# Dense keys and values, and a batch's attention in four groups of 64x64 products

## Chip, cores, metric

One core of a Trainium2 chip runs the whole kernel. The metric is the device time of one execution in microseconds (us), taken over several runs; lower is better.

## What is computed

Eight batches of attention with eight heads each (576 positions, head size 64), then a gated feed-forward block on the 4608 rows of 512 that the heads make together. Heads 0 to 3 see a plain window of the last 32 positions, heads 4 to 7 a window of 128 of which only every fourth position counts.

```python
scores = scale * np.matmul(q, k.transpose(0, 1, 3, 2))
mask_plain = (rel >= 0) & (rel < 32)
mask_dil = (rel >= 0) & (rel < 32 * 4) & (rel % 4 == 0)
attn = softmax(where(mask, scores, -1e9))
x = matmul(attn, v)                       # 4608 x 512 after the heads are put side by side
out = (gelu(x @ w_gate) * (x @ w_val)) @ w_out    # inner width 1536
```

## The kernel before

**Chunks.** The feed-forward block works on nine chunks of 512 rows. Each has a gate stage of 96 matmuls of 512 columns (`ffn1_part`, L636: 12 blocks of the inner width, gate and value, four contraction pieces `kc`) and an output stage of 48 (`ffn2`, L643: four row blocks `tb` of 12). ScalarE (ACT) makes gelu, `g` (L805); VectorE (DVE) multiplies it with the value product, `u` (L810). Results leave through `store` (L651), by ACT (`e`) or DVE (`w`), and a DMA on the SP queue.

**Attention** is done for pairs of heads, called units: unit n belongs to batch n // 4, and each batch has two plain and two dilated units (`pair`, L357: batches 2 and 3 have the dilated ones first). A unit passes these steps, each a letter in the program strings:
- S, scores (L459, L473): 9 blocks of 64 keys by up to 96 queries, for both heads.
- P, the exponential on ACT (L508); M, the mask on DVE (L513).
- D, denominators (L566): a product with ones. N, numerators (L570): a product with the values.
- A, the reciprocal by ln and exp on ACT (L606, L608), or T and B, by transposes on DVE (L594, L611).
- X, the product of numerator and reciprocal into `xT` (L627), one 128-row piece for each unit of a batch: piece `pair(n)` is what the gate matmuls of contraction piece kc read.

**Storage.** For batches 1 to 7, keys and values of the two heads of a unit stand as 128x128 blocks with the heads on the diagonal (or, for odd units, off it: `odd`, L268) and zeros elsewhere. A full 128x128 product then gives both heads. GpSimd (POOL) makes them: `zero` (L199), the spreads (L278 to L289) and the casts of the values (L262), from dense loads. When two units are emitted together (`emit_tiles`, L448), the kernel leaves the zeros out: each product is cut to two 64x64 products, and the even unit uses the diagonal quarters of TensorE, the odd one the other two. Batch 0 has dense keys and uses 64x64 products with a bias for its mask.

**Order.** Nothing is scheduled by a compiler: each engine runs its instructions in the order in which the program gives them. For every chunk c, `gates[c]` and `outs[c]` are strings that `run_program` (L786) walks: a number issues so many matmuls of the chunk's list, `S8@0+S9@6` emits the scores of two units together with their PSUM banks, `e1@2` evicts row block 1 of chunk 2, G and E load ACT's table for gelu or for exp and ln, V, F, H, R start loads. Batch c+1 is computed mostly in the output stage of chunk c; its last numerators, and for batches 6 and 7 more, lie in the gate stages. `firsts` orders the first 16 gate matmuls, so that pieces of `xT` that come late are read late.

**Loads.** Weights come by DMAs on POOL's queue (`load_w`, `load_wo`), with the queries and keys of batches 0 and 1. Values of batch 1 come by SP's queue into `stage` (`load_v`, L245 plain, L250 and L254 dilated); the first of them is held until the second piece of the output weights has landed (`gated`, L163). Later batches: F loads and casts q and k (L291), H transposes them by DMA (L273) and fetches the values (`load_rest`, L317).

**PSUM** has eight banks of 512 columns; gate stages use two pairs of banks in turn, the output stage two, and attention the rest (`win`, `base_of`).

Of the kernel before, what the change touches and what calls it, by code (L numbers as in the profile page):

```python
# [21 lines left out]
def kernel(  # L22
# [29 lines left out]
    NB2 = S // BK  # L52
    BIG = 60000.0
# [19 lines left out]
    ones_two = const.tile([P, P], F16, tag="ones_two")  # L73
# [8 lines left out]

    vraw = [const.tile([P, 4 * NB2 * P], F16, tag=f"v{i}", name=f"v{i}") for i in range(3)]
    qraw = [const.tile([P, 2 * 640 + 8 * NCL + 4 * NB2 * P], F16, tag=f"q{i}", name=f"q{i}") for i in range(2)]
    stage = const.tile([P, 3840], F32, tag="stage")
    s16 = const.tile([P, 4608], F16, tag="s16")
    dense = const.tile([P, 1280 + 8 * NCL], F16, tag="dense")
# [90 lines left out]
    def blocks(t, plain):  # L178

        return t[:, (1 - plain) * 2 * NB2 * P : (2 - plain) * 2 * NB2 * P].rearrange("p (e c) -> p e c", c=P)  # L180

    def views(b):

        raw = qraw[b % 2]
        kt = raw[:, 1280 + 8 * NCL :]
        return (
            raw[:, 0:1280].rearrange("p (g c) -> p g c", g=2),
            raw[:, 1280 : 1280 + 8 * NCL].rearrange("p (g r i) -> p g r i", g=2, r=4),
            blocks(kt, 1),
            blocks(kt, 0),  # L190
            blocks(vraw[b % 3], 1),
            blocks(vraw[b % 3], 0),
        )
# [5 lines left out]
    def zero(t, eng=nc.gpsimd, gs=(0, 1), swap=1):  # L199

        for x in range(2):
            g = gs[0]
            part = t[64 * x : 64 * x + 64].bitcast(F32)
            first = 32 - 32 * (x ^ (g * swap))
            step = NB2 * 64 + swap * (32 if x else -32) * (1 - 2 * g)
            eng.memset(at2(part[:, NB2 * g], first, [[step, len(gs)], [64, NB2], [1, 32]]), 0.0)  # L206
# [49 lines left out]
    def cast_v(dst, i, gs=(0, 1), swap=1):  # L256

        st = st_of(i)[:, 0:1152].rearrange("p (e d) -> p e d", d=D)
        for g in gs:
            for x in range(2):  # L260
                at = slice(NB2 * g, NB2 * g + NB2)
                nc.gpsimd.tensor_copy(dst[half_of(x), at, half_of(x, g * swap)], st[half_of(x), at])  # L262
# [12 lines left out]
    kdp = dense[:, 0:1280].rearrange("p (g c) -> p g c", g=2)  # L275
    kdd = dense[:, 1280 : 1280 + 8 * NCL].rearrange("p (g r i) -> p g r i", g=2, r=4)

    def spread(eng, dst, src, x, g):  # L278

        half = half_of(x)  # L280
        eng.tensor_copy(dst[half, :, :, half_of(x, g)], src[half])  # L281

    def spread_two(dst, src, x):

        half, step = half_of(x), NB2 * P + (-64 if x else 64)
        n = src.shape[2] // 64
        base = dst[half, 0, 64 * x : 64 * x + 1]
        out_ = bass.AP(tensor=base.tensor, offset=base.offset, ap=[base.ap[0], [step, 2], [P, n], [1, 64]])
        nc.gpsimd.tensor_copy(out_, src[half].rearrange("p g (j c) -> p g j c", c=64))  # L289

# [10 lines left out]
    def spread_plain(kp):  # L301
        for x in range(2):
            spread_two(kp, kdp[:, :, 0:S], x)

    def spread_dil(kd, rest):
        for x in range(2):
            for g in range(2):
                spread(
                    nc.gpsimd,
                    kd[:, NB2 * g : NB2 * g + 8].rearrange("p (r i) c -> p r i c", r=4),  # L310
                    kdd[:, g, :, 0:P].rearrange("p r (i c) -> p r i c", c=64),
                    x,
                    g,
                )
            spread_two(kd[:, 8:], rest, x)

    def load_rest(b):  # L317
        qp, qd, kp, kd, vp, vd = tiles["two", b] = views(b)
        turn(qp.rearrange("p g (k c) -> p (g k) c", c=P), s16[:, 0:1280])
        turn(kdp.rearrange("p g (k c) -> p (g k) c", c=P), s16[:, 1280:2560])  # L320
        turn(qd.rearrange("p g r i -> p (g r) i")[:, :, 0:P], s16[:, 2560:3584])
        turn(kdd.rearrange("p g r i -> p (g r) i")[:, :, 0:P], s16[:, 3584:4608])
        for plain in (0, 1):
            load_v(b, 2 - plain, plain)
        spread_plain(kp)
        spread_dil(kd, kdp[:, :, S:640])
        nc.gpsimd.tensor_copy(qd[:, :, :, P:NCL], qp[:, :, S:640].rearrange("p g (i r) -> p g r i", r=4))
        cast_v(vd, 2)
        cast_v(vp, 1)

    def v_first(g):

        dst = vraw[0][:, 2304:3456].rearrange("p (e d) -> p e d", d=D)
        for x in range(2):
            half = slice(64 * x, 64 * x + 64)
            nc.gpsimd.dma_start(
                out=dst[half, 8 * g : 8 * g + 8].rearrange("p (i r) d -> p i (r d)", r=4),
                in_=v[0, HK + 2 * g + x, 0 : 4 * P].rearrange("(i p r) d -> p i (r d)", i=2, r=4),
            )
            if g == 0:  # L340
                nc.gpsimd.dma_start(out=dst[half, 16:18], in_=v[0, HK + x : H : 2, S - 64 : S].rearrange("g p d -> p g d"))
# [35 lines left out]
    def turn_first(n, bank, eng):  # L377
# [11 lines left out]
        if kind:  # L389
            dst = (kdd if t else views(b)[1])[:, hp].rearrange("p r (i e) -> p r i e", e=2)  # L390
            src = col.rearrange("p (e r i) -> p r i e", e=2, r=4)
        else:
            dst = (kdp if t else views(b)[0])[:, hp, 0:S].rearrange("p (i r) -> p i r", r=6)
            src = col.rearrange("p (r i) -> p i r", r=6)
        copy(("dve", "act")[eng], dst, src)
        if kind and t:
            rest = kdp[:, hp, S:640].rearrange("p (i r) -> p i r", r=8)
            copy(("dve", "act")[eng], rest, col.rearrange("p (r i) -> p i r", r=8)[:, 64:R8, :])
        if b and n % 4 == 3:
            if kind:  # L400
                spread_dil(views(b)[3], kdp[:, :, S:640])
            else:
                spread_plain(views(b)[2])
# [4 lines left out]
    def win(n, i):  # L408
        return (2048 + 1024 * i) % 4096 + (0 if is_plain(n) else 80)
# [38 lines left out]
    def emit_tiles(*lists):  # L448

        queues, at = [list(mms) for mms, _ in lists], [0.0] * len(lists)  # L450
        while any(queues):
# [3 lines left out]
            for x in range(2):  # L455
                rows, cols = half_of(x), half_of(x, lists[i][1])
                nc.tensor.matmul(o[cols], lhs[rows, cols], rhs[rows], start=st, stop=end, skip_group_check=True)  # L457

    def two_s_mms(n, bank):  # L459

        b, hp = n // NHP, n % 2
        qp, qd, kp, kd, _, _ = tiles["two", b]
# [3 lines left out]
        for e, c0, t0, w in two_blocks(n):  # L466
            rhs = qp[:, hp, t0 : t0 + w] if is_plain(n) else qd[:, hp, e // 2, t0 - NCL * (e // 2) : t0 - NCL * (e // 2) + w]
            mms.append((psf[:, base + c0 : base + c0 + w], (kp if is_plain(n) else kd)[:, NB2 * hp + e, :], rhs, True, True))
        if not is_plain(n):
            mms.append((psf[:, base + LD - BK : base + LD], kd[:, NB2 * hp + 8, :], qd[:, hp, :, P:NCL], True, True))  # L470
        return mms

    def two_s(n, bank):  # L473

        b, hp = n // NHP, n % 2
        if b:
            emit(two_s_mms(n, bank))
            return
        qp, qd, _, _, _, _ = tiles["two", b]
        base = base_of(n, bank)  # L480
        if ("bias", n) not in tiles:
            bias_first(n, bank)

        def score(c0, w, e, rhs, r=None):
            for x in range(2):
                half = half_of(x)
                if is_plain(n):
                    lhs = kdp[half, hp, BK * e : BK * e + BK]
                elif r is None:
                    lhs = kdp[half, hp, S:640]  # L490
                else:
                    lhs = kdd[half, hp, r, BK * (e % 2) : BK * (e % 2) + BK]
                nc.tensor.matmul(psf[half, base + c0 : base + c0 + w], lhs, rhs[half], start=False, stop=True, skip_group_check=True)

        for e, c0, t0, w in two_blocks(n):
            if is_plain(n):
                score(c0, w, e, qp[:, hp, t0 : t0 + w])
            else:
                r = e // 2
                score(c0, w, e, qd[:, hp, r, t0 - NCL * r : t0 - NCL * r + w], r)  # L500
        if not is_plain(n):
            score(LD - BK, BK, 16 + hp, qd[:, hp, :, P:NCL])
        tiles["S", n] = psf[:, base : base + (LP if is_plain(n) else LD)]
# [16 lines left out]
    def two_mms(n, w0, lhs_of):  # L520
# [3 lines left out]
        ones_of = ones_two if odd(n) else two_ones  # L524
# [45 lines left out]
    def two_num_mms(n, i):  # L570
# [3 lines left out]
        if is_plain(n):  # L574
            return two_mms(n, win(n, i), lambda e: vp[:, NB2 * hp + e, :])
        if b == 0:
            vd = vraw[0][:, 2304:3456].rearrange("p (e d) -> p e d", d=D)
            return two_mms(n, win(n, i), lambda e: vd[:, 16 + hp if e is None else 8 * hp + e % 2 * 4 + e // 2, :])
        return two_mms(n, win(n, i), lambda e: vd[:, NB2 * hp + (8 if e is None else e % 2 * 4 + e // 2), :])

    def two_den(n, i):
        emit(two_den_mms(n, i))

    def two_num(n, i):
        mms = two_num_mms(n, i)
        if n >= NHP or is_plain(n):
            emit(mms)
            return
        for o, lhs, rhs, st, end in mms:
            for x in range(2):  # L590
                half = half_of(x)
# [358 lines left out]
```

The softmax here doesn't subtract the row's maximum and nothing guards it: scores larger than these inputs give would overflow.

## Time and profile before

| what | value |
|---|---|
| time of the runs (median of 3) | 331.09 us (331.04 to 332.13) |
| span of the profiled execution, first to last instruction | 330.3 us |
| granted TensorE clock | 1.000 of full |
| TensorE (PE) matmuls, busy | 322.6 us, 3040 matmuls |
| gate matmuls (L636), output matmuls (L643) | 864 and 420 |
| 64x64 products of pairs of units (L457) | 1182 |
| DVE, ACT, POOL busy | 152.3, 163.2, 149.1 us |
| HBM traffic | 143 GB/s over the span |

The profiled execution's own time was not recorded apart from its span; the runs' times lie about 0.8 us above it, for what lies before the first and after the last instruction. Starts and lengths in the views below are microseconds from the first instruction. Matmuls overlap: one of 512 columns is shown with 0.38 us, while the next starts 0.216 us after it, so that sums are made from starts. "Releaser" is what the last awaited signal came from.

### The profile page before, as it was taken

The page shows a single profiled execution, that of the slowest core. Times are in us where ns is not written, and L with a number is a line of the kernel's source. Part 1 is how long each engine was busy: PE and PEld are TensorE (multiplying, and loading weights), DVE is VectorE, ACT ScalarE, POOL GpSimd, SP SyncE. Part 2 cuts the span into 40 slices and gives each one's busy share as a digit, 9 for nine tenths or more (in the row PEclk, how much of TensorE's full clock was granted, in tenths as well). Part 3 has the DMA queues.
Part 4 walks back from the last instruction along what each step waited for, and adds up shares of the span by engine and source line. Part 5 has one row for each costly group of instructions (what it writes and reads, how often), then busy time and mean ns, then how long its engine had stood idle before and what let it go on. Part 6 is the DMA issues. An engine that isn't in the chain of part 4 may idle for free.

```text
span 330.3 us, 7539 instructions
## 1 busy us (share of the span) xinstructions
PE 322.6 (98%) x3040; PEld 158.0 (48%) x3040; DVE 152.3 (46%) x226; ACT 163.2 (49%) x246; POOL 149.1 (45%) x246
## 2 busy tenths in 40 slices
PE   6899999999999999999999999999999999999996
PEld 4654544444544454444544554444444444444443
DVE  6763653534453344336533568436833533304320
ACT  2663557535763576348733793356334533213322
POOL 8799865499337647536826931476000000000000
PEclk9999999999999999999999999999999999999999
DMA  8999997898797998979879637964000110020002
GB/s 189 196 173 180 202 184 167 248 189 209 172 276 163 200 220 147 260 198 191 234 172 258 147 102 168 239 161 137 34 0 4 73 56 0 0 97 32 0 32 97
DMA packets 109027, 47.98 MB, mean 145 GB/s; under 512 B 83648, under 2 KB 104512, under 8 KB 108992
## 3 DMA queue, kind: packets, MB, share of 16 engines
q1 hardware_dynamic: 97216, 40.06, 50.6%
q0 software_dynamic: 11216, 6.79, 14.5%
q10 hardware_dynamic: 560, 0.66, 0.7%
q8 instruction: 24, 0.39, 0.5%
q14 instruction: 11, 0.09, 0.1%
HBM read 37.75 MB, written 9.44 MB: 143 GB/s over the span
## 4 chain that ended last, share of the span: by engine, by line
PE 83%; DMA 8%; POOL 7%; SPq 1%; issue 0%; DVE 0%; POOLq 0%
PE ps L636 50%; PE ps L643 26%; PE ps L457 5%; DMA wo<-in_moe_w_out_dram 4%; DMA xT<-in_k_dram 2%; DMA stage<-in_v_dram 2%; POOL wv L153 1%; PE ps L446 1%; POOL v L262 1%; POOL xT L176 1%; POOL wg L153 1%; PE ps L667 1%; POOL q L206 1%; POOL v L206 1%; SPq L245 1%
## 5 line engine op out<-in xcount | busy, mean ns | idle before, releaser
L810 DVE SCALAR_TENSOR_TENSOR u_all<-g,ps 128x512 f16<-128x512 f16 x108 | 73.6, 685 | 99.6 <-PE ps L636 92.6
L805 ACT ACTIVATE g<-ps 128x512 f16<-128x512 f32 x108 | 64.0, 597 | 108.7 <-PE ps L636 108.6
L636 PE MATMUL ps<-xT,wg 128*128 128x512 f16 x432 | 114.6, 379 | 0.0
L636 PE MATMUL ps<-xT,wv 128*128 128x512 f16 x432 | 113.5, 379 | 0.0
L643 PE MATMUL ps<-wo,u_all 128*128 128x512 f16 x420 | 98.6, 380 | 0.0
L636 PEld LDWEIGHTS <-wv 128*128 128x128 f16 x432 | 42.1, 98 | 49.9
L636 PEld LDWEIGHTS <-wg 128*128 128x128 f16 x432 | 42.0, 98 | 49.1
L643 PEld LDWEIGHTS <-u_all 128*128 128x128 f16 x420 | 38.2, 98 | 42.1
L262 POOL CAST v<-stage 64x576 f16<-64x576 f32 x60 | 41.4, 690 | 10.4 <-DMA stage<-in_v_dram 7.6
L627 DVE TENSOR_TENSOR xT<-ps,rb 128x576 f16<-128x576 f32 x32 | 29.8, 941 | 22.0 <-PE ps L457 17.9
L221 POOL CAST s<-stage 128x640 f16<-128x640 f32 x24 | 16.9, 732 | 39.4 <-DMA stage<-in_q_dram 26.8
L508 ACT ACTIVATE P<-ps 128x832 f16<-128x832 f32 (+1 forms) x32 | 25.3, 834 | 15.0 <-PE ps L457 12.1
L654 ACT ACTIVATE osb<-ps 128x512 f32<-128x512 f32 x34 | 20.2, 593 | 21.7 <-PE ps L643 21.5
L289 POOL COPY q<-dense 64x1152 f16<-64x1152 f16 (+1 forms) x28 | 20.7, 738 | 12.7 <-DMA dense<-s 6.0
L606 ACT ACTIVATE lg<-ps 128x576 f32<-128x576 f32 x23 | 15.0, 652 | 7.8 <-PE ps L457 6.9
L233 POOL CAST s<-stage 128x512 f16<-128x512 f32 x24 | 14.6, 635 | 9.4 <-DMA stage<-in_q_dram 6.2
L281 POOL COPY q<-dense 64x512 f16<-64x512 f16 x28 | 16.7, 623 | 2.9 <-DMA dense<-s 1.8
L513 DVE TENSOR_TENSOR P<-P,two_d 128x768 f16<-128x768 f16 x14 | 11.2, 825 | 12.8 <-ACT P L508 12.5
L608 ACT ACTIVATE rb<-lg 128x576 f32<-128x576 f32 x23 | 15.7, 683 | 0.7
L513 DVE TENSOR_TENSOR P<-P,two_p 128x832 f16<-128x832 f16 x14 | 10.1, 724 | 11.1 <-ACT P L508 10.9
L457 PEld LDWEIGHTS <-v 64*64 64x64 f16 x460 | 9.3, 107 | 8.8 <-issue 7.0
L457 PE MATMUL ps<-P,v 64*64 64x96 f16 (+5 forms) x460 | 11.4, 199 | 0.4 <-POOL v L262 0.4
(81 smaller groups left out, 180.5 us busy)
## 6 DMA issues: line engine op xcount, KB each, us to landing
out_dram<-osb SPq DMA_DIRECT2D x35, 256.0 KB, 3.1
stage<-in_v_dram SPq DMA_DIRECT2D x32, 144.0 KB, 3.5
stage<-in_v_dram SPq DMA_DIRECT2D x28, 128.0 KB, 2.9
stage<-in_q_dram SPq DMA_DIRECT2D x24, 128.0 KB, 3.6
stage<-in_k_dram SPq DMA_DIRECT2D x24, 128.0 KB, 3.0
stage<-in_q_dram SPq DMA_DIRECT2D x6, 512.0 KB, 4.4
stage<-in_k_dram SPq DMA_DIRECT2D x6, 512.0 KB, 5.3
wg<-in_moe_w_gate_dram POOLq DMA_DIRECT2D x6, 256.0 KB, 6.9
```

What stands on the lines that cost most here:

```text
L221: nc.gpsimd.tensor_copy(s16[:, 1280 * t + 640 * g : 1280 * t + 640 * g + 640].rearrange("p (k c) -> p k c", k=5), st_of(i).rearrange("p (k ...
L262: nc.gpsimd.tensor_copy(dst[half_of(x), at, half_of(x, g * swap)], st[half_of(x), at])
L289: nc.gpsimd.tensor_copy(out_, src[half].rearrange("p g (j c) -> p g j c", c=64))
L457: nc.tensor.matmul(o[cols], lhs[rows, cols], rhs[rows], start=st, stop=end, skip_group_check=True)
L508: nc.scalar.activation(pt[:, 0 : src.shape[1]], src, AF.Exp, bias=0.0, scale=scale)
L513: nc.vector.tensor_tensor(pt, pt, mask, ALU.mult)
L627: nc.vector.tensor_tensor(dst, num, rb, ALU.mult)
L636: nc.tensor.matmul(ps[:, bank, :], w[:, kc, ns], xT[kc][:, tok], start=first, stop=end)
L643: nc.tensor.matmul(ps[:, bank, :], u_all[:, fc, tb * P : (tb + 1) * P], wo_t[fc // 4][:, fc % 4, :], start=(fc == 0), stop=(fc == NNB - 1),)
L654: nc.scalar.activation(osb, ps[:, bank, :], AF.Copy, bias=0.0, scale=1.0 / USCALE)
L805: nc.scalar.activation(g, ps[:, gate_banks(c, args[0])[0], :], AF.Gelu)
L810: nc.vector.scalar_tensor_tensor(u_all[:, nb, :], tiles.pop(("g", nb)), USCALE, val, ALU.mult, ALU.mult)
```

## The change

Batches 1 to 7 keep keys and values dense. The tiles for the zeros, `dense`, `ones_two`, the spreads and the zeroing are gone; `vdiag` holds the one block-diagonal copy that is left, the plain values of batch 0. The DMA transposes write the keys straight to their place. Values are cast in one instruction for 128 rows. The dilated values of batch 1 come by six casting DMAs on POOL's queue.

```diff
-    def cast_v(dst, i, gs=(0, 1), swap=1):
-        st = st_of(i)[:, 0:1152].rearrange("p (e d) -> p e d", d=D)
-        for g in gs:
-            for x in range(2):
-                at = slice(NB2 * g, NB2 * g + NB2)
-                nc.gpsimd.tensor_copy(dst[half_of(x), at, half_of(x, g * swap)], st[half_of(x), at])
+    def cast_v(dst, i):
+        nc.gpsimd.tensor_copy(dst, st_of(i)[:, 0:1152].rearrange("p (e d) -> p e d", d=D))
...
-        turn(kdp.rearrange("p g (k c) -> p (g k) c", c=P), s16[:, 1280:2560])
+        turn(kp.rearrange("p g (k c) -> p (g k) c", c=P), s16[:, 1280:2560])
...
-        spread_plain(kp)
-        spread_dil(kd, kdp[:, :, S:640])
...
+    def v_cast(b, g, rest=False):
+        dst = views(b)[5][:, NB2 * g : NB2 * g + NB2]
         for x in range(2):
+            half = half_of(x, b and g)
             nc.gpsimd.dma_start(
+                out=dst[half, 0:8].rearrange("p (i r) d -> p i (r d)", r=4),
+                in_=v[b, HK + 2 * g + x, 0 : 4 * P].rearrange("(i p r) d -> p i (r d)", i=2, r=4),
             )
...
     def second():
         load_w(4)
-        for t in views(1)[2:]:
-            zero(t)
...
         wo1 = [load_wo(i) for i in range(3)][1]
+        v_cast(1, 0, True)
+        v_cast(1, 1)
         two_masks()
...
         load_v(1, 1, True)
-        load_v(1, 2, False)
     def second_v():
-        for t in views(2)[2:4]:
-            zero(t)
...
         cast_v(views(1)[4], 1)
-        cast_v(views(1)[5], 2)
```

All products of batches 1 to 7 are 64x64, those of the denominators with a plain block of ones, and they are always emitted for two units. ln and exp (A) are split into two words, l and r, and take the place of T and B for these batches.

```diff
-                nc.tensor.matmul(o[cols], lhs[rows, cols], rhs[rows], start=st, stop=end, skip_group_check=True)
+                nc.tensor.matmul(o[cols], lhs[rows], rhs[rows], start=st, stop=end, skip_group_check=True)
...
-        ones_of = ones_two if odd(n) else two_ones
+        ones_of = two_ones if n < NHP else ones[:, 0:BK]
...
+    def two_l(n):
+        c0 = tiles["den", n]
+        lg = nrm.tile([P, S], F32, tag="lg", bufs=2)
+        nc.scalar.activation(lg, psf[:, c0 : c0 + S], AF.Ln)
+        tiles["lg", n] = lg
+    def two_r(n):
+        rb = nrm.tile([P, S], F32, tag="rb", bufs=3)
+        nc.scalar.activation(rb, tiles.pop(("lg", n)), AF.Exp, scale=-1.0)
+        tiles["rb", n] = rb
```

The strings of the chunks are made by two functions. A batch's attention is whole in the output stage of chunk c; with i, j, k, l its four units, the groups stand where the words with + stand, and y, z, 0, 2, 4 are banks (the last digit of a two-digit place picks an offset, `win`).

```diff
+    def win(n, at):
+        bank, kind = at // 10, at % 10
+        return 512 * bank + ((0, 832, 960) if is_plain(n) else (80, 880, 880))[kind]
...
-        low = ((0, 1), (2, 3))
+        low = ((0, 1), (6, 7) if c else (2, 3))
...
+        loads = {1: "F3", 2: "R", 3: "F5 H5", 4: "F6 H6", 5: "F7 H7"}.get(c, "")
+        rest = " ".join(f"4 g{nb} 4 u{nb}" for nb in range(2, NNB - 1))
+        before = f"e3@{c - 1}" if 1 < c < NCH - 1 else ""
+        return f"{before} {loads} 8 G {'5 g0 1 u0 1 g1 1 u1' if c == 1 else '2 g0 2 u0 2 g1 2 u1'} {rest} 4 g{NNB - 1} 4" + (f" u{NNB - 1}" if c > 6 else "")
...
+    def out_words(c):
+        if c == 0:
+            return (
+                "V1 F2 S4@4+S5@6 1 E P4 10 P5 1 M4 S6@4+S7@6 M5 1 P6 6 P7 M6 3 D4@40+D5@60 l4 l5 M7 r4 r5 6 w2@0 4 w0@0 4 "
+                "w1@0 H2 N4@50+N5@20 D6@52+D7@22 X4 l6 X5 l7 r6 r7 10 N6@20+N7@40 X6 X7 2 e3@0"
+            )
+        if c > 6:
+            return "12 e0 12 e1 12 e2 12 w3" if c < NCH - 1 else "12 e0 12 e1 12 e2 L"
+        i, j, k, l = (NHP * (c + 1) + n for n in range(NHP))
+        y, z = (0, 3) if c % 2 else (5, 2)
+        return (
+            f"1 u11 4 S{i}@{y}+S{j}@{z} E P{i} P{j} M{i} M{j} 7 e0 5 S{k}@{y}+S{l}@{z} D{i}@{y}1+D{j}@{z}1 P{k} P{l} M{k} M{l} "
+            f"7 e1 l{i} l{j} r{i} r{j} 10 N{i}@{y}0+N{j}@{z}0 D{k}@{y}2+D{l}@{z}2 X{i} X{j} 2 e2 l{k} l{l} r{k} r{l} "
+            f"10 N{k}@20+N{l}@40 X{k} X{l} 2"
+        )
+    orders = {
+        0: "000 100 002 102 010 110 012 112 001 101 011 111 003 103 013 113",
+        1: "000 001 010 011 002 012 100 101 110 111 102 112 003 013 103 113",
+        2: "002 003 012 013 102 103 112 113 000 001 010 011 100 101 110 111",
+        3: "000 001 010 011 100 101 110 111 002 003 012 013 102 103 112 113",
+    }
+    firsts = {c: orders[c if c < 3 else 2 if c == 3 else 3] for c in range(NCH)}
```

Before, the output stage of chunk 1, for comparison, had six places with attention products, and the last numerators (N11) stood in the gate stage after it:

```python
"1 u11 5 S8@0+S9@6 1 E P8 10 P9 M8 1 S10@0+S11@4 e0@1 M9 1 P10 4 P11 D8@1 M10 2 A8 1 M11 3 N8@0+D9@1 "
"e1@1 1 A9 X8 7 e2@1 1 N9@1+D10@0 1 A10 X9 8 N10@0+D11@1 1 A11 X10"
```

## Prediction

> **What bounds the kernel now.** First the page: busy time, the forty slices, the summary of the chain.
>
> ```profile
> span 330.3 us, 7539 instructions
> PE 322.6 (98%) x3040; PEld 158.0 (48%) x3040; DVE 152.3 (46%) x226; ACT 163.2 (49%) x246; POOL 149.1 (45%) x246
> ...
> PE   6899999999999999999999999999999999999996
> ...
> PE 83%; DMA 8%; POOL 7%; SPq 1%; issue 0%; DVE 0%; POOLq 0%
> ```
>
> PE is full from the third slice to the last; no other engine is half busy. The DMA and POOL shares of the chain are one early stretch, read below. The view of waits gives PE one wait after the first 17 us: 0.4 us for `POOL v L262`. So the time falls by PE time taken out, less new holes in PE's queue.
>
> What is PE time? Chunk 7's gate stage holds no attention: its 96 matmuls start at 264.99 and the next stage at 285.71, so one 512-column matmul costs 20.72/96 = 0.2158 us. The last four gate matmuls of chunk 0 start at 40.89. From there to 264.99 lie 4 + 7x48 + 6x96 = 916 such matmuls, 197.7 us of the 224.1. **Attention of batches 1 to 7 costs the other 26.4 us.**
>
> Next the timeline of PE in chunk 1's output stage (start, length, work; lengths overlap, so I use starts):
>
> ```profile
> 77.18 1.46 PE L643 MATMUL ps<-wo,u_all 128*128 128x512 f16 x6
> 78.57 0.54 PE L457 MATMUL ps<-q 64*64 64x96 f16 x36
> 79.03 2.76 PE L643 MATMUL ps<-wo,u_all 128*128 128x512 f16 x12
> 81.73 0.56 PE L457 MATMUL ps<-q 64*64 64x96 f16 x36
> 82.22 1.25 PE L643 MATMUL ps<-wo,u_all 128*128 128x512 f16 x5
> 83.31 0.50 PE L446 MATMUL ps<-P,two_ones 128*128 128x288 f16 x6
> 83.67 1.46 PE L643 MATMUL ps<-wo,u_all 128*128 128x512 f16 x6
> ```
>
> Six matmuls from 77.18 fill PE to 78.47; the next output matmul starts at 79.03, so the first group of 64x64 products costs 0.56, the second 0.60. It waits 0.10 going in and about as long coming out. The lone denominator at 83.31 stays in 128x128 mode and costs 0.37. So I split a group into a **stream of 0.37** and a **switch of about 0.21**. Counting groups through the stages I get 36 tiled and 12 wide: 48 streams x 0.375 + 36 switches x 0.21 = 25.6. With the hole below (0.7) that is 26.3, against 26.4 measured.
>
> **The change, part by part.**
>
> *Groups.* Each batch now has two score pairs, two denominator pairs, two numerator pairs: 6 streams. Chunk 0 has five groups; chunks 1 to 6 four each (scores; scores and denominators; numerators and denominators; numerators). That is 42 streams and 29 switches: 42x0.375 + 29x0.21 = 21.8. Saved: 6 streams (2.2), 7 switches (1.5), the old hole (0.7): **4.4 us**. No row has a group of 60 to 68 products. The longest is this one:
>
> ```profile
> 226.05 1.47 PE L643 MATMUL ps<-wo,u_all 128*128 128x512 f16 x6
> 227.44 0.55 PE L457 MATMUL ps<-P,v 64*64 64x96 f16 x40
> 227.93 3.20 PE L643 MATMUL ps<-wo,u_all 128*128 128x512 f16 x14
> ```
>
> 40 products cost 0.59 with the switch, 12 ns each inside: a second list behind it costs 0.37 if that pace holds. The slow end is the run of 64 transposes at 39.07 to 40.23, 18 ns each: 64 x 6 ns = 0.4 more per long group, 13 groups, 5 us. Below zero it cannot go, since the columns are the same. I take the 12 ns row, the same kind of work.
>
> A rule speaks against this. The Trainium skill, TensorEngine Tiling (Array Packing), Restrictions and Gotchas, says that different row tiles cannot use one PSUM bank at the same time. Here units of a pair write both row halves into the same bank, and the group above still takes 0.38 us inside for 40 products; by the rule a stream would be 0.75, and the 48 streams of now alone 36 us, more than all attention costs, so the row decides.
>
> *Block-diagonal copies.* POOL loses the zeroing (L206, 11 us in the groups of POOL), the spreads (L281 and L289, 37 us), and of 60 value casts (41 us) it keeps 4 and gets 13 wide ones, some 19 us: 70 of its 149 us. None of it is on PE's path after 57 us (PE waits for nothing there), so it is worth nothing directly. In chunk 0 the fetch of batch 2 (H2) now stands behind three stores on SP and is called 12 matmuls later; SP issued its last value load at 77.8 (timeline of SP), which makes a cast by some 82, and its first numerators come at 77.2 + 34x0.2158 + 1.5 = 86. That cover of 4 us is what H2 may lose; any more would stop PE. The six added load issues (0.62 each) on POOL stand where 4.8 us of memsets stood, ahead of the masks, which were ready at 37.7 for a use at 44.
>
> *Batch 1's values, the one place with a price.* Three views: the timeline of POOL, the chain in order of time, the timeline of PE.
>
> ```profile
> 49.21 0.66 POOL L262 CAST v<-stage 64x576 f16<-64x576 f32 x1 [2.45 <-DMA stage<-in_v_dram]
> 50.12 0.67 POOL L262 CAST v<-stage 64x576 f16<-64x576 f32 x1 [0.26 <-DMA stage<-in_v_dram]
> 52.05 1.39 POOL L262 CAST v<-stage 64x576 f16<-64x576 f32 x2 [1.26 <-DMA stage<-in_v_dram]
> ```
> ```profile
> 31.75 12.65 DMA wo<-in_moe_w_out_dram
> ...
> 46.43 5.56 DMA stage<-in_v_dram
> ```
> ```profile
> 53.49 0.23 PE L457 MATMUL ps<-P,v 64*64 64x96 f16 x1 [0.41 <-POOL v L262]
> ```
>
> The plain values wait (L245, held for the second `wo` load) until 44.40, land to 51.99, are cast to 53.44. Before, unit 4 needed only the first half, at 50.94; unit 5 waited (52.74 due, 53.49 run). Now one cast of 128x1152 needs all four landings, and N4 and N5 stand together behind 36 output matmuls. From the output stage's first matmul: 42.36 + 36x0.2158 + scores 0.56 + denominators 0.58 + 0.10 = **51.4**. When are the values ready? The eight memsets that leave POOL's start (4.8 us) let the queue fill sooner, but the weight loads land one every 1.3 to 1.7 us without a break, so the queue is limited by its rate, and I give `wo` 0.5 us. Behind it come six new loads of dilated values, some 0.3 MB, 1.5 us at the 190 to 200 GB/s of these slices, which share the engines with the plain values. So landing near 51.7. The cast: 64x576 takes 0.66 and 128x640 0.72 us, so by elements 1.2 to 1.3. Ready at 52.9: a hole of **1.5 us**; 3.0 if the new loads are served first in full, 0 if `wo` lands 2 us sooner. Queued behind N4 and N5 is everything on PE, so it counts in full.
>
> *The moved softmax.* All units now use ln and exp on ACT:
>
> ```profile
> L608 ACT ACTIVATE rb<-lg 128x576 f32<-128x576 f32 x23 | 15.7, 683 | 0.7
> L606 ACT ACTIVATE lg<-ps 128x576 f32<-128x576 f32 x23 | 15.0, 652 | 7.8 <-PE ps L457 6.9
> ```
>
> 23 become 30, seven DVE transposes go. ACT holds 4 exps (3.3), three evictions (1.8), eight of these (5.1 in sequence) and a table load (1.28) per output stage, 11.5 of 13.4 us: enough, but serial. I walk a chunk from its first output matmul. Scores i,j at 1.2, exps to 3.3; scores k,l at 4.3, denominators at 4.8 (masks done 4.2 to 4.6); ln and exp of i,j 7.5 to 10.0; N i,j at 9.0, D k,l ends 9.8; eviction 10.4 to 11.0; ln k,l to 12.35; N k,l, whose banks these must leave, at 12.5. Slack there: 0.1 us. Multiplies of i,j end at 11.9, 0.6 early. After N k,l come two output and eight gate matmuls (2.2 us) before the third `xT` piece is read. The multiplies start 0.7 after N: plain 0.76 each is in time; the dilated ones (1.13 in the timeline of DVE) end about 0.2 late in chunks 3 to 6. I put **0.7 us** on this in all; the ends are 0 and 0.6 in each of six chunks, 3.6.
>
> The end of chunks 7 and 8 has other banks and order, the same matmuls, and two banks in turn as before: nothing, in lack of a wait to move. Batch 0 keeps its products: nothing.
>
> **Sum:** -4.4 + 1.5 + 0.7 = -2.2 us on the profiled 330.3, so 328.1 there. The runs' median is 331.09, 0.8 above the span for what lies around it: **328.9**.
>
> **Rivals.** (a) The hole for the values closes and slack holds: -4.4 and a little, 326.7 to 327.3. For it: the copies vanish and loads shift forward; against it: the early queue is rate-limited. (b) The chain on ACT and DVE is later than my walk by 0.3 in each of six stages: 1.8 more, 330.7, no difference that can be told. For it: slack of 0.1; against it: no wait on ACT in PE's view today. (c) **Slower: long groups run out of queued instructions.** If the groups of 60 to 68 run at the transposes' 18 ns, 13 groups x 0.4 = 5 us: 328.9 + 5 = 333.9. It decides from 0.3 us per long group on (3.9 us from the forecast to 0.5% slower, over 13). Against it: the 40 products show no slowing at their end. The order of groups is written out in the diff, so that the change does not do what it says is no case of its own.
>
> **Numbers.** Forecast 0.50, (a) 0.17, (b) 0.15, (c) 0.18. A measurement here tells 0.5% (1.65 us) from no change. The forecast's own spread, 327.3 to 330.5, lies for some seven tenths below 329.4: faster 0.35 + 0.17 = 0.52, same 0.15 + 0.15 = 0.30, slower 0.18. The range goes from 326.5 (no hole at all) to 332.3 (hole at 3.0 and late softmax together); what it leaves out is (c).
>
> **What would show it.** The timeline of PE in chunks 1 to 6: four groups, 0.56 to 0.60 for pairs and 0.95 for the mixed ones; 1.3 or more refutes the streams and is (c). A wait of PE for `POOL v` near 51.4, ending near 53. Waits of PE for ACT `lg` before the last numerators, or for DVE `xT` at the tenth gate matmul, each 0.2 or less; 0.5 or more in every chunk is (b). I am wrong in sign if the first stage, not PE, sets later stages: loads that come late for batches 2 or 3.

## The result, and the profile after

| what | before | after |
|---|---|---|
| median of 20 runs each | 331.36 us (331.04 to 332.64) | 330.98 us (329.69 to 332.82) |
| ratio after / before | | 0.9983, 95% interval 0.9968 to 0.9998 |
| span of the profiled execution | 330.3 us | 329.5 us |
| its granted clock | 1.000 | 0.995 |
| matmuls on PE | 3040 | 3167 |

The change made the kernel faster by 0.17%, less than the 0.5% that a measurement here can tell; 0.66% was forecast. In the runs with a span on record the time is 1.65 to 1.87 us above it. The prediction took 0.8, because the profiled execution of before was a late one (330.3; the median spans of its later runs are 329.5 to 330.1). Three executions of before that took 620 to 673 us are left out of every comparison below.

The page after, the same lines as before, with the clock row:

```profile
span 329.5 us, 7661 instructions
...
PE 321.6 (98%) x3167; PEld 156.7 (48%) x3167; DVE 137.3 (42%) x208; ACT 169.4 (51%) x258; POOL 82.0 (25%) x130
...
PEclk9799999999999999999999999999999999999999
...
PE 82%; DMA 13%; POOL 2%; SPq 1%; issue 0%; ACT 0%; DVE 0%; POOLq 0%; ACTq 0%
```

POOL lost 67 us of work and the span 0.8. In the clock row the second slice is at 0.7; before, all were at 0.9 or more. The chain has more DMA (13% for 8%): more of it runs through loads (by its list of lines `stage` 4% for 2%, `wv` 3% where none stood among the first).

The timeline of PE in chunk 1's output stage, after:

```profile
80.19 0.54 PE L418 MATMUL ps<-q 64*64 64x96 f16 x36
80.65 2.76 PE L590 MATMUL ps<-wo,u_all 128*128 128x512 f16 x12
83.35 0.56 PE L418 MATMUL ps<-q 64*64 64x96 f16 x36
83.74 0.53 PE L418 MATMUL ps<-P,ones 64*64 64x96 f16 x24
84.20 3.84 PE L590 MATMUL ps<-wo,u_all 128*128 128x512 f16 x17
87.98 0.55 PE L418 MATMUL ps<-P,v 64*64 64x96 f16 x40
88.38 0.55 PE L418 MATMUL ps<-P,ones 64*64 64x64 f16 x20
88.86 2.76 PE L590 MATMUL ps<-wo,u_all 128*128 128x512 f16 x12
91.56 0.60 PE L418 MATMUL ps<-P,v 64*64 64x96 f16 x40
```

Four groups. Inside the mixed ones the second list starts 0.39 to 0.40 after the first, with no switch between. So this part does what was foreseen; the rest was lost elsewhere.

**Where the time went.** The next profile, `a_again`, is the same kernel in a second execution, at full clock. From start to start of the stages' first matmuls, against before (chunk 0, for example, from 42.36 to 56.09 before and from 42.05 to 57.52 after):

| stretch | before | after, full clock | difference |
|---|---|---|---|
| chunk 0, output stage to next gate stage | 13.74 | 15.47 | +1.73 |
| chunk 1, gate stage | 21.08 | 21.08 | 0.00 |
| chunk 1's output stage to chunk 7's | 208.53 | 205.53 | -3.00 |
| chunk 7's output stage and chunk 8's gate stage | 31.08 | 31.08 | 0.00 |
| last output stage to the end | 13.55 | 13.90 | +0.35 |
| sum | | | -0.92 |

Six chunks give 3.0 us, about as foreseen. Chunk 0 and the last stage take 2.1 back. The table compares one execution of each kernel; the medians agree with it, since the full-clock runs of the change (next section) have a median of 330.36 against 331.36 for all of before's, 1.0 us less.

### The profile page after: what moved, and what is told of

Its sections match the earlier page's. It is cut to its first block, busy times and chain, and to the rows that moved or that the text cites. A ratio compares the mean times of both kernels' runs of the same rounds, so it can differ in the third digit from the quotient of the medians.

```text
span 329.5 us, 7661 instructions
## 1 busy us (share of the span) xinstructions
PE 321.6 (98%) x3167; PEld 156.7 (48%) x3167; DVE 137.3 (42%) x208; ACT 169.4 (51%) x258; POOL 82.0 (25%) x130
## 4 chain that ended last, share of the span: by engine, by line
PE 82%; DMA 13%; POOL 2%; SPq 1%; issue 0%; ACT 0%; DVE 0%; POOLq 0%; ACTq 0%
PE ps L583 50%; PE ps L590 25%; PE ps L418 5%; DMA wo<-in_moe_w_out_dram 4%; DMA stage<-in_v_dram 4%; DMA wv<-in_moe_w_val_dram 3%; DMA u_all<-in_q_dram 2%; SPq L234 1%; PE ps L614 1%; POOL wg L153 1%; ACT lg L545 0%; POOL wv L153 0%; POOL v L247 0%; DVE xT L574 0%; POOL vdiag L254 0%
## 5 line engine op out<-in xcount | busy, mean ns | idle before, releaser
L590 PE MATMUL ps<-wo,u_all 128*128 128x512 f16 x420 | 97.0, 380 | 0.0
L247 POOL CAST v<-stage 128x1152 f16<-128x1152 f32 x13 | 15.1, 1163 | 69.5 <-DMA stage<-in_v_dram 69.5
L601 ACT ACTIVATE osb<-ps 128x512 f32<-128x512 f32 x31 | 18.6, 599 | 20.9 <-PE ps L590 20.5
L545 ACT ACTIVATE lg<-ps 128x576 f32<-128x576 f32 x30 | 18.2, 650 | 5.3 <-DVE xT L574 3.8
L551 ACT ACTIVATE rb<-lg 128x576 f32<-128x576 f32 x30 | 19.0, 688 | 0.1
L453 DVE TENSOR_TENSOR P<-P,two_p 128x832 f16<-128x832 f16 x14 | 8.4, 604 | 13.8 <-ACT P L448 12.5
L453 DVE TENSOR_TENSOR P<-P,two_d 128x768 f16<-128x768 f16 x14 | 7.7, 558 | 14.2 <-ACT P L448 11.4
L418 PEld LDWEIGHTS <-q 64*64 64x64 f16 x576 | 8.3, 110 | 6.8 <-issue 5.9
L418 PEld LDWEIGHTS <-v 64*64 64x64 f16 x600 | 7.5, 107 | 7.0 <-issue 5.0
L418 PE MATMUL ps<-q 64*64 64x96 f16 (+2 forms) x576 | 10.5, 207 | 0.3 <-DVE q L333 0.3
```

The source lines that it names most:

```text
L418: nc.tensor.matmul(o[cols], lhs[rows], rhs[rows], start=st, stop=end, skip_group_check=True)
L453: nc.vector.tensor_tensor(pt, pt, mask, ALU.mult)
L545: nc.scalar.activation(lg, psf[:, c0 : c0 + S], AF.Ln)
L551: nc.scalar.activation(rb, tiles.pop(("lg", n)), AF.Exp, scale=-1.0)
L590: nc.tensor.matmul(ps[:, bank, :], u_all[:, fc, tb * P : (tb + 1) * P], wo_t[fc // 4][:, fc % 4, :], start=(fc == 0), stop=(fc == NNB - 1),)
L601: nc.scalar.activation(osb, ps[:, bank, :], AF.Copy, bias=0.0, scale=1.0 / USCALE)
```

## The experiments

The theory after the result: grouping saves 0.5 us in each of chunks 1 to 6; chunk 0 gives it back, because the values of batch 1 come when they come. Rivals: the spread of the runs hides the gain; longer groups or the softmax on ACT eat it; the masks or the gated loads are late.

**Repetition: `b_again`, `a_again`.** Both kernels unchanged.

> The kernel before, unchanged, to see how its spans and clocks scatter. If the one profiled execution (span 330.3) was a late one, the spans of these runs gather near 329.6 and the step that failed is the baseline of my sum. If it was typical, they gather near 330.3. If the half clock of the first 20 us is the change's doing, no run here shows a mean clock under 0.999; if it falls by chance, some do, and they are 1 to 2 us longer.

> The changed kernel, unchanged. By the theory that the change saves 2.4 us after the first 42 us and loses it by the clock at the start, runs of clock 1.000 have a span near 328.2 and those of 0.995 near 329.7 and more. By the rival that the clock does not matter, both have the same span.

Measured: before against itself 0.9994 (0.9979 to 1.0008), after 0.9989 (0.9973 to 1.0005). So the difference is a fraction of a per cent. The spans of before gather at 329.5 (median), so its profiled execution was a late one. The runs of after fall into two kinds: of its 32 unchanged runs here and in the result, 12 had a granted clock of 0.995 or less, called low here; of the 78 runs of before with a clock on record, 6. In the 20 of the result the 12 others have a median of 330.36, the 8 at low clock 331.97. But the full-clock runs of `a_again` have a median span of 329.15, not the 328.2 of the expectation: the clock alone doesn't take the gain.

The next view is PE of `a_again` around the denominators and numerators of chunk 0:

```profile
47.96 3.20 PE L590 MATMUL ps<-wo,u_all 128*128 128x512 f16 x14
53.05 0.58 PE L418 MATMUL ps<-P,v 64*64 64x96 f16 x40 [1.89 <-POOL v L247]
53.46 0.53 PE L418 MATMUL ps<-P,ones 64*64 64x96 f16 x24
53.92 2.33 PE L590 MATMUL ps<-wo,u_all 128*128 128x512 f16 x10
56.18 0.23 PE L418 MATMUL ps<-P,v 64*64 64x96 f16 x2
56.60 0.54 PE L418 MATMUL ps<-P,v 64*64 64x96 f16 x38 [0.19 <-ACT lg L545]
```

The fourteen output matmuls end near 51.1. Then PE stands until 53.05, for the one wide cast of the values, here in the timeline of POOL:

```profile
51.84 1.15 POOL L247 CAST v<-stage 128x1152 f16<-128x1152 f32 x1 [4.33 <-DMA stage<-in_v_dram]
```

PE was due there at 51.16, and the values were ready at 52.99. A second hole follows at 56.18, some 0.4 us: two of the last numerators' products run, the others wait for an `ln` (tile `lg`). The same execution, ACT and DVE:

```profile
54.93 0.65 ACT L545 ACTIVATE lg<-ps 128x576 f32<-128x576 f32 x1 [4.51 <-DVE xT L574]
55.90 0.65 ACT L545 ACTIVATE lg<-ps 128x576 f32<-128x576 f32 x1 [0.32 <-issue]
```
```profile
54.07 1.42 DVE L574 TENSOR_TENSOR xT<-ps,rb 128x576 f16<-128x576 f32 x2 [2.19 <-PE ps L418]
```

The `ln` of unit 6 waits for the multiply of unit 4 on DVE (54.07, 0.77 long by the chain of waits). By the offsets in `win`, N4 at place 50 runs from bank 5 into bank 6, where D6 (place 52) begins, and N5 and D7 meet in bank 3 in the same way; no columns overlap. That the shared bank is why ACT's read stands behind DVE's is read from the program: no run gives the two windows banks of their own. For the second `ln` the trace names no releaser of its 0.32 ("issue"); by the banks it stands behind unit 5's multiply. The second hole thus hangs on the first, since these multiplies begin only when N4 and N5 have run.

**The clock at the start: `b_fill`, `a_fill`.** Three 512-column matmuls of ones stand where PE waits near 12 us.

```diff
-                "t6@1@1 t7@0@0 S1@6 ..."
+                "t6@1@1 W3@3@0 t7@0@0 S1@6 ..."
```

> Before, with three 512-column products of ones (0.65 us) between the transposes t6 and t7, where TensorE waits 0.75 us for keys. If idle time there is what lowers the clock, no run is under 0.999 and the spread of the times shrinks to under 0.8 us; the median falls by as much as such runs were frequent (0 to 0.7 us). If idle time there has nothing to do with it, spread and clock stay.

> The changed kernel with the same three products, where its profile shows 1.10 us of idle time ahead of the half clock. By the theory the clock stays at 1.000 and the median falls from 331.0 by 0.7 us or more to 330.0 or less, 1.0 us or more under before with the same filler. By the rival (the low clock comes from elsewhere) it stays at 331.0 with as many runs of 0.995.

Measured: before with filler 1.0006 (0.9996 to 1.0016), after with filler 0.9979 (0.9960 to 0.9998). Low clock in 0 of 11 and 2 of 12 runs: rarer than without the filler (12 of 32), but on too few runs to tell. The median of after stays at 330.98, where 330.0 or less was expected; the hole is 1.89 us in this profile too, which starts its first gate matmul 0.7 us later. The filler moves nothing that can be told from `a_again`.

**Units 6 and 7 first: `a_swap`.** The dilated values of batch 1, which come by their own DMAs, are used first; the plain ones get ten output matmuls and two more streams of time. It also moves the masks ahead of the value loads and orders the first gate matmuls accordingly.

```diff
-  "... S4@4+S5@6 ... S6@4+S7@6 ... N4@50+N5@20 D6@52+D7@22 X4 l6 X5 l7 r6 r7 10 N6@20+N7@40 X6 X7 2 e3@0"
+  "... S6@4+S7@6 ... S4@4+S5@6 ... N6@50+N7@20 D4@52+D5@22 X6 l4 X7 l5 r4 r5 10 N4@20+N5@40 X4 X5 2 e3@0"
```

> The changed kernel, but in chunk 0 the dilated units 6 and 7 come first (their values land by 48.3 us and need no cast), the plain ones last; the masks are made ahead of the six value loads on POOL's queue; chunk 1's gate reads the dilated pieces first. Theory: the hole ahead of batch 1's first numerators (1.9 us in the full-clock profile) is what eats the gain, so it goes, and chunk 0 from its first output matmul to chunk 1's first gate matmul falls from 15.5 us to 13.6 or less; the runs' median falls by 1.5 to 2.2 us to about 329. Rival, that the loads only move the wait to another place (keys of batch 2, the last numerators): chunk 0 gets shorter but a wait of the same size shows up before 80 us, and the median stays within 0.5 us of 331.0.

Measured: 329.19 us, 0.9909 (0.9884 to 0.9935). Chunk 0 takes 13.99 (13.6 or less was expected), and chunk 1's gate stage 20.72 for 21.08. In PE's timeline:

```profile
52.77 0.55 PE L418 MATMUL ps<-P,v 64*64 64x96 f16 x40
53.17 0.55 PE L418 MATMUL ps<-P,ones 64*64 64x64 f16 x20
...
56.76 0.58 PE L418 MATMUL ps<-P,v 64*64 64x96 f16 x38 [0.62 <-ACT lg L545]
```

No wait for `POOL v` is left, but this profile alone doesn't show why: its start was a late one (clock 0.995), and `a_split` below, late too and with the old order of units, has no such wait either. The runs show it (median 1.8 us below the change's, full-clock runs 1.5 to 2.0: about the hole), and `a_best`, with this order, has no such wait at full clock. The wait for `lg` has grown to 0.62.

**The masks alone: `a_masks`.** The line `two_masks()` stands ahead of the two `v_cast(1, ...)`.

> The changed kernel with the masks made ahead of the six value loads on POOL. In the changed kernel each of these loads stood still until the DMA eight places before it had landed, and the masks came at 42 to 48.6 us instead of 33 to 37.7. Theory: TensorE waited for no mask, so the time stays within 0.3 us of 331.0 and the hole for the values at 1.9 us. Rival: the loads of the values land later by the masks' 5 us, or the masks were late for the denominators: 0.5 us or more either way.

Measured: 0.9980 (0.9963 to 0.9997), hole 1.54, chunk 0 15.13. Nothing that can be told from the change; so `a_swap` gained by the order of units (with the order of the gate matmuls that goes with it), not by the masks.

**The gate of the loads: `a_gate0`.** The plain values of batch 1 are held for the first piece of the output weights instead of the second.

```diff
-        wo1 = [load_wo(i) for i in range(3)][1]
+        wo1 = [load_wo(i) for i in range(3)][0]
```

> The changed kernel with one edit: the plain values of batch 1 are held for the landing of the first piece of the output weights and not the second, 2 to 2.7 us earlier. Theory (the hole ahead of the numerators is a landing and nothing else): it shrinks from 1.9 us to 0.6 or less and the median falls by 0.8 to 1.3 us to about 330. Rival (the queues share the engines, so the weights' second and third piece land later by what the values gain): TensorE waits for the weights in the output stage of chunk 0 instead, and the median stays at 331.0.

Measured: 0.9983 (0.9964 to 1.0001). The four loads went out at 41.0 to 43.0 instead of 44.1 to 46.8 and landed at 48.1, 50.9, 51.6 and 52.2; in `a_again` at 49.2, 50.0, 50.9 and 51.7. The hole was to shrink to 0.6; it didn't, since the last of them comes no earlier:

```profile
53.56 0.58 PE L418 MATMUL ps<-P,v 64*64 64x96 f16 x40 [2.05 <-POOL v L247]
53.98 0.85 PE L418 MATMUL ps<-P,ones 64*64 64x96 f16 x24
54.76 3.64 PE L590 MATMUL ps<-wo,u_all 128*128 128x512 f16 x10
```

What the plain values were given early, others lost: the third piece of `wo` landed at 47.16 for 46.47 in `a_again`, the last of the six dilated loads at 50.69 for 48.27. So the landing of the last is set by the bytes that share the engines, not by the gate; that PE would wait for the weights instead, as the rival had it, did not happen. And after the hole ten output matmuls take 3.64 us, in `a_again` 2.33: the clock went down. The Trainium skill, DMA: Bandwidth & Descriptors, Queues, rings and completion order, says that each DMA engine goes round-robin between the queues that have work; that agrees with these landings.

**Groups apart: `a_split`.** One output matmul between the two lists of the mixed groups, in chunks 1 to 6: twelve more switches.

```diff
-  7 e0 5 S{k}+S{l} D{i}+D{j} ... 10 N{i}+N{j} D{k}+D{l} ...
+  7 e0 4 S{k}+S{l} 1 D{i}+D{j} ... 9 N{i}+N{j} 1 D{k}+D{l} ...
```

(The places behind @ are left out.)

> The changed kernel with one output matmul between the two halves of each mixed group of chunks 1 to 6, so 12 more switches of mode and nothing else. My price of 0.2 us for a switch gives 12 x 0.2 = 2.4 us: from chunk 1's first output matmul to chunk 7's 205.5 becomes 207.9. If a long group of 60 products pays for its length (rival c), less: 12 x 0.05 or none.

One run, of low clock at its start but not in these chunks: chunks 1 to 6 take 208.06 us, 2.53 more than in `a_again`, 0.21 for each switch. PE's timeline, with the scores and the denominators of the second group apart:

```profile
82.53 0.56 PE L418 MATMUL ps<-q 64*64 64x96 f16 x36
83.03 0.39 PE L590 MATMUL ps<-wo,u_all 128*128 128x512 f16 x1
83.35 0.55 PE L418 MATMUL ps<-P,ones 64*64 64x96 f16 x24
83.83 3.63 PE L590 MATMUL ps<-wo,u_all 128*128 128x512 f16 x16
```

The output matmul at 83.03 fills 0.22, so the denominators behind it cost 0.58, a stream and a switch.

**Storage without grouping: `d_old`.** Dense keys and values and their loads as in the change, with the banks, strings and reciprocals of before (T and B for half of the units).

> Storage and loads of the changed kernel with the order, the banks and the groups of before: dense keys and values, but the units that stood alone are now 64x64 products of one unit. Theory (the gain after 57 us is the grouping, not the storage): from chunk 1's first output matmul to chunk 7's the 208.5 us of before grow by the 10 lone groups' switches, 10 x 0.2, to 210.5; the numerators of batch 1 stand at 51 us and wait for the one wide cast to 53; in all 333 to 335 us. Rival (the gain comes with the lighter POOL and the dense storage): 208.5 falls to 206 or less.

Measured: 336.72 us, 1.0144 (1.0104 to 1.0183), more than the 333 to 335 expected; two of its four runs had a low clock. Chunks 1 to 6 take 210.76 us, 2.2 more than before, for ten such groups: the lone denominators and numerators, 128x128 before, are now 64x64 and pay a switch.

```profile
83.87 1.25 PE L588 MATMUL ps<-wo,u_all 128*128 128x512 f16 x5
85.05 0.53 PE L416 MATMUL ps<-P,ones 64*64 64x288 f16 x12
85.52 1.47 PE L588 MATMUL ps<-wo,u_all 128*128 128x512 f16 x6
```

Five matmuls fill 1.08, so this group costs 0.57 where the same one cost 0.37 before. Chunk 0 has the hole as well (2.05). So dense storage in the old order is slower, and the gain is the grouping's.

**The end: `a_lane`.** The last stores of chunks 6 and 7 go as two DMAs, which gives the last DMA of the kernel another completion semaphore.

```diff
-        nc.sync.dma_start(out=out[t0 : t0 + P, :], in_=osb)
+        cuts_ = 2 if 6 <= c <= 7 and 4 * c + tb > 24 else 1
+        for i in range(cuts_):
+            cols = slice(i * DM // cuts_, (i + 1) * DM // cuts_)
+            nc.sync.dma_start(out=out[t0 : t0 + P, cols], in_=osb[:, cols])
```

> The changed kernel with seven of the late stores (chunk 6 row blocks 1 to 3, chunk 7 all) cut into two DMAs each, so that the last DMA has another place in the row of semaphores that SP tests at the end. Theory: the tail from chunk 8's first output matmul to the end falls from 13.90 us back to 13.5, since SP no longer has eight tests of 0.06 us to do after the last landing. Rival, that the tail's 0.36 us came from the DMA or the eviction: it stays at 13.90.

One run: last output stage to the end 13.47 us, 0.43 less; 13.46 in `a_best`, which has this edit too. Issue of the last store in the timelines of before, `a_again` and `a_lane`:

```profile
327.70 0.38 ACTq L679 DMA_DIRECT2D out_dram<-osb  x1
```
```profile
326.13 0.38 ACTq L626 DMA_DIRECT2D out_dram<-osb  x1
```
```profile
327.22 0.38 ACTq L629 DMA_DIRECT2D out_dram<-osb  x1
```

The spans end at 330.33, 329.12 and 329.78: 2.63, 2.99 and 2.56 us after it. Up to this issue the stage takes 10.91 us in all three, and the DMA lands 1.63 to 1.64 us after it; the difference lies behind the landing: 1.00, 1.36 and 0.93 us. There SP tests the kernel's semaphores in a fixed row, in the trace some 0.06 us each. In the change the last DMA's stands second, so that the rest of the row comes after its landing; before, and in `a_lane`, it was among the last.

**Together: `a_best`.** The edits of `a_swap` and `a_lane`, and four output matmuls moved from ahead of N6 and N7 to behind D4 and D5 (`w1@0` with them), which gives `ln` more time.

> The version with dilated units first and early masks, with two more edits: the last numerators of chunk 0 stand 14 output matmuls behind the group before them (w1@0 moved between), where the profile showed a wait of 0.6 us for the logarithm that clears their bank, and the late stores cut in two as in the run on the tail. Theory: chunk 0 falls from 14.0 to 13.4 us, the tail from 13.90 to 13.5, the median from 329.2 to 328.4 or less. Rival, that one of the two only moves a wait: 329.0 or more.

Measured: 327.82 us (327.71 to 329.40), 0.9890 (0.9872 to 0.9908), the fastest of all. Chunk 0, here at full clock, takes 13.24 us and no hole is left in it:

```profile
50.30 0.55 PE L418 MATMUL ps<-P,v 64*64 64x96 f16 x40
50.70 0.55 PE L418 MATMUL ps<-P,ones 64*64 64x64 f16 x20
51.18 3.20 PE L590 MATMUL ps<-wo,u_all 128*128 128x512 f16 x14
54.31 0.67 PE L418 MATMUL ps<-P,v 64*64 64x96 f16 x40
```

## Why the prediction was wrong, point by point

The mechanism was right: the grouping saves what its prices say. Three terms of the sum were not. The 1.5 us for the hole was taken as the whole price of chunk 0 and of the gate stage behind it, which came to 1.25 us more than the prices give; the end was put at nothing and cost 0.35; the clock had no term and took some 0.4 on the mean.

- **Groups: right.** Chunks 1 to 6 hold 864 matmuls of 512 columns, 186.5 us at 0.2158. Attention there cost 208.53 - 186.5 = 22.1 and now costs 205.53 - 186.5 = 19.1. By the prediction's prices, 36 streams and 24 switches are 18.5. `a_split` gives the switch again, 0.21.
- **Rival (c), long groups: refuted.** The second list starts 0.4 after the first in every mixed group. The rule on PSUM banks that the prediction weighed would have doubled the streams; no run shows that. (Its 36 us for the rule counts the twelve 128x128 groups as well; without them it is 36 x 0.75 + 12 x 0.375 = 31.5, still more than 26.4.)
- **The moved softmax: 0.7 was too much.** The 19.1 are 0.5 above the 18.5, but before stood 0.2 above its prices as well (22.1 against 41 streams and 31 switches, 21.9). That leaves 0.3 for the softmax and all else, and the view of waits names no wait of PE for ACT or DVE between 62 and 326 us; the one group out of line is chunk 5's second, 1.10 for 0.95. With it rival (b) falls. This slip was on the safe side and hid a part of the others.
- **The copies: right.** POOL's 67 us were worth nothing by themselves (`d_old`: 2.2 more in chunks 1 to 6, what its ten switches cost). One remark failed: the masks did not stay ahead. In POOL's timeline of the change:

```profile
24.60 0.75 POOL L153 DMA_DIRECT2D wv<-in_moe_w_val_dram  x1 [0.46 <-DMA wv<-in_moe_w_val_dram]
...
42.70 0.59 POOL L294 DMA_DIRECT2D v<-in_v_dram  x1 [3.17 <-DMA wo<-in_moe_w_out_dram]
43.33 0.82 POOL L311 COPY two_p<-band 64x768 f16<-64x768 f16 x1
```

From 24.6 on each issue waits for the landing of the DMA eight places before it (the trace has eight completion semaphores in turn for POOL's DMAs, 109 to 116, and each issue waits for its own), so the six new loads hold POOL until 43.3, and the masks, done at 37.7 before, come between 43.3 and 48.6. `a_masks` shows that this costs nothing that can be told.
- **Batch 1's values: the hole was right, what hangs on it was not.** Forecast 1.5; the full-clock profiles have 1.52 (`a_lane`), 1.54 (`a_masks`) and 1.89 (`a_again`, `a_fill`), so rival (a), in which it closes, falls. Landing (51.69 for 51.7) and cast (ready at 52.99 for 52.9) came as forecast; in `a_again` the hole is longer because PE came earlier (51.16 for 51.4). In before, too, what PE has earlier there comes back as a wait: it reaches its output stage 0.62 earlier than `b_fill` does, and its next gate stage at the same time (56.09 and 56.10). The step that failed is to take this hole as the whole price of chunk 0. It did not follow the holding of banks behind the hole: the second hole costs 0.4 in chunk 0. Nor the start of the next gate stage: that stage lost a lone numerator group of 0.36 and yet takes 21.08 as before, since two gate matmuls wait 0.2 each (at 58.55 and 61.34), by the times and the program's order the first for DVE's late multiply, the second for the first gelu.
- **The end: "the same matmuls ... nothing".** The matmuls are the same; the end came 0.35 later, by the place of one semaphore (`a_lane`).
- **The clock: not foreseen.** In the profile of the change PE waits 1.10 us at 11.1, and then runs slow. First the change's profile, then `a_again`'s, then `a_lane`'s:

```profile
12.24 0.62 PE L351 MATMUL ps<-ident,xT 72*64 72x72 f16 x16 [1.10 <-DMA xT<-in_k_dram]
12.79 0.90 PE L418 MATMUL ps<-q 64*64 64x96 f16 x18
```
```profile
11.58 0.56 PE L418 MATMUL ps<-q 64*64 64x96 f16 x18
```
```profile
12.11 0.45 PE L351 MATMUL ps<-ident,xT 72*64 72x72 f16 x16 [0.86 <-DMA xT<-in_k_dram]
12.49 0.56 PE L418 MATMUL ps<-q 64*64 64x96 f16 x18
```

The same 18 products take 0.90 for 0.56. The trace's record of the granted clock has one stretch at half, from 12.36 to 15.78; the first gate matmul comes 1.5 us later than in `a_again`. This is also why the change's own profile flatters it: PE came late to the values, and its hole was only 0.7. The Trainium skill, TensorE: Matmul & The Clock Gate, Part 1: The HAM clock gate, has the clock halved after an idle window of about 3.4 us; here a wait of 1.10 was followed by half speed, and one of 0.86 in `a_lane` was not.

The sum, at full clock and from chunk 0's output stage on: by the prediction's prices (its 0.7 for the softmax included), against the measured stages of before, 0.84 for chunk 0, -0.36 for gate stage 1 and -2.84 for chunks 1 to 6, together -2.36 us; measured -0.92. The difference of 1.44 is 0.89 in chunk 0 (0.4 longer hole, 0.4 second hole), 0.36 in gate stage 1, 0.35 at the end, less 0.16 in chunks 1 to 6. That `a_again` came to this stage 0.31 earlier than before did is not in the sum; the longer hole took most of it back. The low-clock runs, 12 of 32 for 6 of 78 at 1.1 to 1.5 us each, take about 0.4 more on the mean: -0.5, against -0.56 measured (0.17% of 331.4; interval -1.1 to -0.1). The budget closes within the interval; the clock's part is counted from runs, not tested alone.

**Open.** Why the change falls into the low clock more often was not settled. The hole in chunk 0 is one place where it happens (`a_gate0`), the wait near 12 us another (also in the profiles of `a_swap` and `a_split`). Idle time alone doesn't decide it: the holes of 1.89 in `a_again` and `a_fill` and of 2.05 in `d_old` were followed by full clock, the one of 2.05 in `a_gate0` by half. The clock records give a hint. In each of the four profiles the half-clock stretch is 3.41 us long, and it begins a whole number of such lengths after the record does (2, and 14 in `a_gate0`), at another time of the kernel in each execution. Cut into steps of this length, the trace of `a_gate0` has its whole hole in the step ahead of the half clock, that of `d_old` has its hole across a border, 0.97 and 1.08. So where a wait falls among these steps seems to count as much as its length; no run tests that.

## What to carry to other kernels

Price a regrouping in the stages that repeat, and then walk the first and the last stage on their own: there a landing or a fixed chain sets the end, and every microsecond that PE saves ahead of such a landing comes back as a wait. Where one operand comes late, use it last: the order of units gained some four times what the change did (`a_swap`: 0.9909 against 0.9983). After placing a wait, follow what it delays behind it, through shared PSUM banks too, and read the start from more than one execution.

## What the runs showed of the hardware

- A switch into and out of 64x64 products costs 0.21 us, and lists of different operands behind each other share one (`a_split`: 12 more switches, 2.53 us).
- POOL's DMAs take eight completion semaphores in turn here, so the ninth issue waits for the first to land. A timeline of before had shown it already (an issue at 12.39 waits 1.26 us for a load eight places earlier).
- An earlier issue doesn't land earlier where the engines are full: the first 3 us sooner, and the last landing 0.5 us later (`a_gate0` against `a_again`).
- After waits of 0.84 to 2.05 us PE's granted clock was half for 3.41 us in four profiles (the change's, `a_swap`, `a_split`, `a_gate0`); after waits of 0.86 to 2.05 us in others it did not.
- The row of semaphore tests at the end costs 0.4 us or nothing, by where the last DMA's stands (1.36 us from landing to end in `a_again`, 0.93 in `a_lane`).
